# Two-layer decode block: two folded weight chunks as one transfer each, and some projection rows placed later

## The chip, the cores and the metric

The kernel runs on one core of a Trainium2 chip. Its time is the device time of one execution in microseconds (us), from a program that is launched once and reads all of its inputs from device memory. The core has five engines that this text names: PE (TensorE, matmuls; PEld are its weight loads), DVE (VectorE), ACT (ScalarE), POOL (GpSimd) and SP (SyncE, which here only issues transfers). Transfers run on 16 DMA engines beside them.

## The reference

Two blocks, A (attention over a cache) and B (a small MLP), are applied in turn, and the pair is run twice with the same weights and the same cache. The activation has 8 batch rows of one token with 448 numbers.

```python
x = x + _A_ref(_layernorm(x), A_k_cache, A_v_cache, A_wq, A_wo)
x = x + _B_ref(_layernorm(x), B_w1, B_w2, B_w3, B_w4)
x = x + _A_ref(_layernorm(x), A_k_cache, A_v_cache, A_wq, A_wo)
x = x + _B_ref(_layernorm(x), B_w1, B_w2, B_w3, B_w4)

def _A_ref(x, k_cache, v_cache, wq, wo):     # x: 8 x 1 x 448
    q = (x @ wq).reshape(B, Sq, 16, 256)      # 16 query heads, 8 cache heads, 4096 positions
    scores = einsum("bhqd,bhkd->bhqk", q, k) * 256 ** -0.5
    o = einsum("bhqk,bhkd->bhqd", softmax(scores), v)
    return o.reshape(B, Sq, 4096) @ wo

def _B_ref(x, w1, w2, w3, w4):                # one token: the shifted groups are zero
    x1 = x + hs
    return x1 + _gelu(_layernorm(x1) @ w3) @ w4
```

With one token per row, the four groups of B's first part are shifted out of the sequence, so `hs` is zero and `w1` and `w2` are not read. K and V of one batch row and one cache head are 4096 x 256 numbers of bf16, 2 MB each; there are 8 x 8 such pairs. Both layers use the same cache.

## The kernel before

**Rows and layers.** The kernel works through the batch rows. For each row b it runs layer 0 (all 8 cache heads) and then layer 1 on the same cache. Heads 0 to 2 are the "free" heads: their K and V are loaded once for each layer. Heads 3 to 7 are "kept": parts of their K (head 7: one quarter) and of V (heads 6 and 7) stay on chip from layer 0 to layer 1, and layer 1 begins with them.

**Cache slots.** The cache lives in 30 slots of 512 KB (`QUARTERS`); a K or V tile of 2 MB is four units. SP loads one to four neighbouring units by one transfer, if that many neighbouring slots are free. A slot comes free when PE has used the unit for the last time, by a score (L1136 or L1378) or by the product with the probabilities (L1262).

**One head.** `front` loads K, turns it by PE (L1482) with copies back by DVE and ACT (L1413, L1414), scores it with the two queries (L1378 by rows, L1136 by columns), and makes the softmax's probabilities. `back` loads V, multiplies (L1262), copies out (L1276, L1278), sums (L1286), scales into `oT` (L1292, two buffers) and multiplies by the head's part of `wo`: `wo_row`, four matmuls on L1312, which add to one row of the PSUM tile `psR`. When most heads of a row (seven, as a rule) have been added, `turn` (L1074, L1077) turns the row into a column.

**The MLP.** After layer 0's attention of row b, `mid(b)` runs block B on one column: L907 (`w3`), L1053 (`w4`), then the second layer's queries (L891, `wq`). Beside that chain run the backs of the next row's free heads, whose V is loaded in single units (`MOST = 1`).

**The weights.** 448 = 3 x 128 + 64. The last 64 rows of `wq` (4096 columns) and `w3` (1792 columns) are folded: their left half lies in partitions 0 to 63 of `wqx_sb` and `w3x_sb`, their right half in 64 to 127. Each half is a transfer of its own (L1546 to L1549, L1556, L1557); the second half of `wq`'s is issued by ACT, everything else that is large by SP (L626 for weights, L643 for the cache).

**The order of the work.** It is not written by hand. Every operation is handed to a planner (`Plan.schedule`) with an estimated duration and a priority, the smaller the earlier. `CH` puts the chain operations first, `hi` (the operation's number less 100,000) comes next, and scores and most products have their own number. The planner walks a model of the engines in time and fixes the order on each engine; the waits are derived from it. For the cache loads it keeps SP's order and chooses when each load is issued, how many units it joins and in which slots. `next_kv` waits for as many neighbouring free slots as the load would like, until `LEAD` (3.5 us) before the modelled end of what is already queued; then it takes the largest fit that there is. `ISSUE` (4.0 us) is the modelled time from an issue to the first data. While PE would idle, the planner places filler matmuls (L1689).

Of the kernel before, what the change touches and what calls it, by code (L numbers as in the profile page):

```python
# [6 lines left out]
P = 128  # L7
B = 8
D = 448
# [43 lines left out]
Q1 = 176  # L53
ROWS = True
SHORT = 0.1


class Op:
# [28 lines left out]
class Plan:  # L87
# [5 lines left out]
    HOT = 3500  # L93


    ISSUE, LEAD = 4.0, 3.5
    BLOCK, FETCH = 128, 6.0
    LAT = {"pe": 0.25, "dve": 0.06, "act": 0.06, "pool": 0.05, "sp": 0.4}

# [374 lines left out]
def bass_interleave_layers__gqa_block_cached__mixer_s_mlp__decode_kernel(  # L474
# [20 lines left out]
    plan = Plan()  # L495
# [6 lines left out]
    def sb(name, shape, dt):  # L502
        n = 4 if dt in (f32, i32) else 2
        for s in shape[1:]:
            n *= s
        al = 32 if n >= 128 else 8
        cursor[0] = (cursor[0] + al - 1) // al * al
        t = nc.alloc_sbuf_tensor_at(name, shape, dt, offset=cursor[0], align_bytes=al)
        cursor[0] += (n + al - 1) // al * al
        assert cursor[0] <= high0, (name, cursor[0], high0)  # L510
        return t

    wq_sb = sb("wq_sb", [P, 3, 4096], bf)
    wqx_sb = sb("wqx_sb", [P, 2048], bf)
    wo_sb = sb("wo_sb", [P, 32 * D], bf)
    w3_sb = sb("w3_sb", [P, 3, F], bf)
    w3x_sb = sb("w3x_sb", [P, F // 2], bf)
# [105 lines left out]
    def dma(name, dst, src, nbytes, sem, val, wr, at, row=8192):  # L623

        us = nbytes / 16 / 26.88e3 + nbytes / row / 16 * 0.008
        plan.op("sp", lambda eng: eng.dma_start(dst, src), us / FASTER, name, wr=wr, prio=at,  # L626
                dma=(sem, val))

    def dma_once(name, parts, keys, at, also=()):

        for i, (dst, src, nbytes, *row) in enumerate(parts):
            dma(name, dst, src, nbytes, nc.alloc_semaphore(f"s_{name}{i}"), 16,
                [keys[i], *(also if i == 0 else ())], 4 * at - 0.5, *row)
# [3 lines left out]
    def issue_kv(o, n, q):  # L637
# [6 lines left out]
        o.dma = (slot_sem[q], 16 * slot_n[q])  # L644
        o.dur = ((n << 15) / 26.88e3 + 8 * 0.008) / FASTER + SHORT * (n < 3)

# [36 lines left out]
    def const_c(v):  # L683
# [7 lines left out]
            wr=["sel"])  # L691
# [7 lines left out]
    for bank, key in [(psR, "R"), (psM, M)]:  # L699
        plan.op("dve", lambda v, bank=bank: v.memset(bank[:, :], 0.0), 0.5, "const",  # L700
                wr=["psM", ("row", 0), ("row", 1)], banks=[key])
    for i in range(2):
        plan.op("dve", lambda v, i=i: v.memset(psP[i][:, 0:DH], 0.0), 0.3, "const", wr=["pz"],
                banks=[f"P{i}"])
# [9 lines left out]
    def pe(fn, n, rd=(), wr=(), banks=(), name="chain", prio=None, width=20):  # L714

        if prio is None:
            prio = urge[0] + len(plan.ops)
        d = 0.06 + 0.026 * n
        return plan.op("pe", fn, (d, max(d, 0.06 + n * width / 1200), width * n, n), name, rd=rd, wr=wr, banks=banks, prio=prio)
# [152 lines left out]
    def q_mms(t, mts, rhs, bank, at, step, copies):  # L872

        last = None
        for i, mt in enumerate(mts):
            hq, c = mt // 2, mt % 2
            for kc in range(4):


                if kc < 3:
                    w = wq_sb[:, kc, hq * 256 + c:hq * 256 + 256:2]
                    r = rhs(kc)
                else:
                    o = (hq % 8) * 256
                    w = wqx_sb[:, o + c:o + 256:2]
                    r = rhs(3 + hq // 8)
                if step == 1:
                    r = bcast(r, copies, 1)  # L890
                last = t.matmul(bank[:, at + i * step:at + i * step + copies], w, r,  # L891
                                start=(kc == 0), stop=(kc == 3))
        return last

    def h_mms(t, rhs, bank, at, step, copies, mts=range(14)):

        last = None
        for mt in mts:
            for kc in range(4):

                g = mt % 7
                c = slice(g // 2 * 256 + g % 2, g // 2 * 256 + 256, 2) if g < 6 else slice(768, 896)
                w = w3_sb[:, kc, mt // 7 * 896:mt // 7 * 896 + 896][:, c] if kc < 3 else w3x_sb[:, c]
                r = rhs(kc if kc < 3 else 3 + mt // 7)
                if copies > step:
                    r = bcast(r, copies // step, 1)
                last = t.matmul(bank[:, at + mt * step:at + mt * step + copies], w, r,  # L907
                                start=(kc == 0), stop=(kc == 3))
        return last

    W4 = ["w40", "w41", "w42", "w43"]
    W3 = ["w30", "w31", "w32", "w3x0", "w3x1"]

    def column_sums():

# [2 lines left out]
        for g in range(4):  # L918
            pe(lambda t, g=g: q_mms(t, range(8 * g, 8 * g + 8), one, psM, SC, 1, QW), 32,
               rd=["mask"] + WQ, wr=["psM"], banks=[M], prio=len(plan.ops), width=QW)  # L920

# [5 lines left out]
    def column_sums_h():  # L927
        def one(kc):
            return mask[:, kc:kc + 1]
        pe(lambda t: h_mms(t, one, psM, SC, 1, HW), 56, rd=["mask"] + W3, wr=["psM"], banks=[M],  # L930
           prio=len(plan.ops), width=HW)
        dv(lambda v: v.tensor_single_scalar(cs_h[:, :], psM[:, SC:SC + 14], 1.0 / D, ALU.mult), rd=["psM"], wr=["cs_h"], banks=[M],
           prio=len(plan.ops))

    WQ = ["wq0", "wq1", "wq2", "wqx0", "wqx1"]

    def last_rows(src, skey, n):

# [37 lines left out]
    def mlp(src, skey, n, dst, dkeys, rows_open=False):  # L976
# [12 lines left out]
        if dst is None:  # L989
            shift(0, mom[:, 2, 2:3], rsy[:, 1, B - 2:B - 1], [("s", 0), ("y", 1, B - 2)])  # L990
            last_stats(1)
            pe(lambda t: h_mms(t, lambda kc: src[:, kc, 2:2 + n], ch, at, n, HW // 2), 56,
               rd=[*skey] + W3, wr=[kb], banks=[bk], width=HW)
            for r in range(n):
                scaled(r, rsy[:, 1, B - 2 + r:B - 1 + r], [("y", 1, B - 2 + r)])
        elif few:
# [9 lines left out]
            for mts in H_PARTS:  # L1006
                pe(lambda t, mts=mts: h_mms(t, lambda kc: src[:, kc, 0:n], ch, at, n, HW, mts), 4 * len(mts),
                   rd=[skey] + W3, wr=[kb], banks=[bk], width=HW)
            variance(st, False, v0, ["st"], "v0", sbank)
# [4 lines left out]
        else:  # L1014
            norm(src, skey, True, n)
            pe(lambda t: h_mms(t, lambda kc: yb6[:, kc, 0:n], ch, 0, n, n), 56,
               rd=KH + W3, wr=[kb], banks=[bk])
            dv(lambda v: v.tensor_copy(h_, ch[:, 0:m]), rd=[kb], wr=KH, banks=[bk])
# [217 lines left out]
    def back(layer, b, h):  # L1236
# [10 lines left out]
        hi = len(plan.ops) - 10 ** 5  # L1247
# [6 lines left out]
        for u in range(4):  # L1254

            def pv(t, u=u, q=vs[u]):
                last = None
                for s in range(8):
# [10 lines left out]
                    wr=[("pv", par, x) for x in range(u, 4)], banks=[bk], prio=first)  # L1269
            if u == 0:  # L1270
                o.tbank = bk
            if u not in keep_v:
# [7 lines left out]
                banks=[bk], prio=hi)  # L1280

        def sum_mm(t):
# [8 lines left out]
           prio=hi)  # L1291
# [3 lines left out]
            wr=[("oT", no)], banks=[bk], prio=hi).tbank = bk  # L1295
# [10 lines left out]
        if k <= turn_at:  # L1306
            def wo_row(t):
                last = None
                for i in range(4):
                    a = (4 * h + i) * D  # L1310
                    r = 64 * layer + 32 * (i % 2)
                    last = t.matmul(psR[r:r + 1, 0:D], oT[no][:, i % 2, i // 2:i // 2 + 1],  # L1312
                                    wo_sb[:, a:a + D], start=(k == 1 and i < 2),
                                    stop=(k == turn_at and i >= 2),
                                    skip_group_check=True, tile_position=(0, r))
                return last
            o = plan.op("pe", wo_row, (0.41, 0.78, 448, 4), "wor", rd=[("oT", no), "wo0"], wr=[kr],
                        banks=["R"], prio=hi)
            if k == HOTK and layer == 0:
                o.hot = True  # L1320
        xkeys = [ok] + (["x3all" if b < B - 2 else ("xf", b - B + 2)] if layer else [])
        if k == turn_at:
            for a, mts in [(0, range(2)), (2 * P, range(2, NC5))]:
                w = min(2 * P, D - a)
                dv(lambda v, a=a, w=w: v.tensor_copy(oW[:, 0, 0:w], psR[:, a:a + w]), 0.42, rd=[kr],
                   wr=REG, banks=["R"], name="acc", prio=hi)
# [4 lines left out]
                def turn(t, a=a, mts=mts):  # L1331
# [7 lines left out]
                   prio=hi, width=YW)  # L1339
# [188 lines left out]
    def second_queries(b, h, prio):  # L1528

        src = x2c[b % 2]  # L1530
        pe(lambda t: q_mms(t, range(4 * h, 4 * h + 4), lambda kc: src[:, kc, 0:1], psM, SC,
                           1, QW), 16, rd=[("x2", b)] + WQ, wr=["psM"], banks=[M], prio=prio, width=QW)
        dv(lambda v: v.scalar_tensor_tensor(
# [9 lines left out]
    def load_wq():  # L1543
        dma_once("wq", [(wq_sb[:, kc, :], A_wq[kc * P:(kc + 1) * P, :], 1 << 20)
                        for kc in range(3)], ["wq0", "wq1", "wq2"], 2)
        dma_once("wqx", [(wqx_sb[0:64, :], A_wq[384:D, 0:2048], 1 << 19)], ["wqx0"], 0.05)  # L1546
        s_wqx = nc.alloc_semaphore("s_wqx1")
        plan.op("act", lambda a: a.dma_start(wqx_sb[64:P, :], A_wq[384:D, 2048:4096]), 0.1, "wqx1",
                wr=["wqx1"], prio=0, dma=(s_wqx, 16))  # L1549

    def load_rest():
        dma_once("wo", [(wo_sb[:, :].rearrange("p (t n) -> p t n", n=2 * D),
                         A_wo.rearrange("(t m c) n -> m t (c n)", m=P, c=2), 3670016, 1792)], ["wo0"], 6)
        dma_once("w3", [(w3_sb[:, kc, :], B_w3[kc * P:(kc + 1) * P, :], 458752)
                        for kc in range(3)], ["w30", "w31", "w32"], 18)
        dma_once("w3x", [(w3x_sb[0:64, :], B_w3[384:D, 0:896], 114688 * 2),  # L1556
                         (w3x_sb[64:P, :], B_w3[384:D, 896:1792], 114688 * 2)], ["w3x0", "w3x1"], 18)  # L1557
    def load_w4():
        w4s = B_w4.rearrange("(s f) n -> s f n", s=2)
        dma_once("w4", [(w4_sb[:, 7 * i * D:(7 * i + 6) * D].rearrange("p (t n) -> p t n", n=2 * D),  # L1560
# [5 lines left out]
    def first_queries():  # L1566
# [11 lines left out]
        for h in range(8):  # L1578
            pe(lambda t, h=h: q_mms(t, range(4 * h, 4 * h + 4), lambda kc: yb[:, kc, :], psM,
                                    Q1 + 32 * h, B, B), 16, rd=YB + WQ, wr=["psM", "q1"], banks=[M])  # L1580
        first_q(0, None)
# [4 lines left out]
    free_heads = list(range(HKV - KEEP_K))  # L1586
# [19 lines left out]
    def run(tasks):  # L1606
        for t in tasks:
            (fronts_of if t[0] == "f" else back)(*t[1:])
# [31 lines left out]

    load_wq()
    load_rest()
    first_queries()
    load_w4()
# [104 lines left out]
```

## Time and profile before

| what | value |
|---|---|
| median of 3 runs | 1085.01 us (1085.01 to 1085.93) |
| the profiled execution's own time | 1082.09 us |
| its span, first to last instruction | 1080.2 us |
| mean granted TensorE clock | 0.937 |
| busy: PE, PEld, DVE, ACT, POOL | 943.6, 651.1, 598.8, 339.3, 97.9 us |
| read from device memory | 434.18 MB |
| cache loads of SP: 2 MB, 1.5 MB, 1 MB, 512 KB | 137, 25, 22, 141 |
| projection rows on PE (L1312) | 444 matmuls, 65.1 us |

A profile is one execution. The page gives busy time and share for each engine, then the span in 40 slices of 27 us, with the busy share in tenths, the DMA engines' share and what they moved. "DMA queue" lines give packets, megabytes and the time that the packets took as a share of 16 engines. "DMA issues" lines give transfer, issuing queue, count, size and the median time from issue to landing. A wait line reads: who waited, for whom, us in total, times, the longest. In a timeline line the first two numbers are start and length in us. A line number such as L1312 is a line of the kernel before.

### The profile page before, as it was taken

Reading aid. Unit: us, or ns where it says so; the run is one execution under the profiler, and the core shown is the slowest. Engines: PE = TensorE matmul, PEld = TensorE weight load, DVE = VectorE, ACT = ScalarE, POOL = GpSimd, SP = SyncE. Lnnn points to the kernel's source line nnn. Section 1 sums busy time; section 2 is a strip of 40 time slices with the busy share of each in tenths; the row PEclk is TensorE's granted clock in tenths of the full one; section 3 lists DMA queues with packets and bytes.
Section 4 is the critical chain, followed back from the end, with each engine's and each line's share of the span. In section 5 each row is a group of like instructions: output and inputs, shape, how many; then the busy total and the mean of one; then the engine's idle time right before and its main releaser. Section 6 shows DMA issues by size and latency. Waiting matters only on the chain.

```text
span 1080.2 us, 33935 instructions
## 1 busy us (share of the span) xinstructions
PE 943.6 (87%) x15144; PEld 651.1 (60%) x15144; DVE 598.8 (55%) x1895; ACT 339.3 (31%) x940; POOL 97.9 (9%) x278
## 2 busy tenths in 40 slices
PE   5889798988988889898898989998889999998895
PEld 4556556665656656566566655666556675666663
DVE  3345445555665556455565555565556655565564
ACT  1235113341234403254023531334214341343150
POOL 0000000000110101011010100101001000110010
PEclk9899989998999989999899998999989997999895
DMA  9999999999999999999999999999999999999994
GB/s 356 407 428 420 392 380 424 426 397 410 388 425 425 421 404 413 424 427 418 385 409 427 423 415 388 427 425 423 402 389 426 426 407 398 399 427 418 348 422 189
DMA packets 51342, 436.38 MB, mean 404 GB/s; under 512 B 5486, under 2 KB 8700, under 8 KB 27260
## 3 DMA queue, kind: packets, MB, share of 16 engines
q1 hardware_dynamic: 51108, 433.95, 97.9%
q8 instruction: 119, 1.95, 0.7%
q10 hardware_dynamic: 88, 0.26, 0.1%
q14 instruction: 27, 0.22, 0.1%
HBM read 434.18 MB, written 0.01 MB: 402 GB/s over the span
## 4 chain that ended last, share of the span: by engine, by line
DMA 50%; PE 39%; DVE 5%; issue 2%; SPq 1%; ACT 1%; POOL 0%; POOLq 0%; DVEq 0%
DMA kv<-in_A_k_cache_dram 27%; DMA kv<-in_A_v_cache_dram 22%; PE psT L1482 14%; PE psP L1262 7%; PE psT L1378 6%; PE psM L1136 3%; PE psM L891 2%; PE psR L1312 2%; PE psM L1053 1%; SPq L626 1%; DMA w_sb<-in_B_w_dram 1%; DVE kv L1413 1%; DVE oS L1276 1%; DVE oS L1278 1%; PE psP L1286 1%
## 5 line engine op out<-in xcount | busy, mean ns | idle before, releaser
L1482 PE MATMUL psT<-ident_f,kv 128*128 128x128 f32 x2752 | 376.3, 285 | 21.6 <-DMA kv<-in_A_k_cache_dram 19.3
L1482 PEld LDWEIGHTS psT<-ident_f,kv 128*128 128x128 f32 x2752 | 305.7, 144 | 101.2 <-issue 55.2
L1413 DVE COPY kv<-psT 128x512 f32<-128x512 f32 x381 | 260.8, 690 | 180.9 <-PE psT L1482 173.3
L1414 ACT COPY kv<-psT 128x512 f32<-128x512 f32 x339 | 197.5, 586 | 389.4 <-PE psT L1482 301.1
L1262 PE MATMUL psP<-kv,pT 128*2 128x256 bf16 x4096 | 178.3, 289 | 17.9 <-DMA kv<-in_A_v_cache_dram 14.5
L1378 PE MATMUL psT<-kv,qz 128*32 128x512 bf16 x1664 | 135.9, 399 | 6.3 <-ACT kv L1414 4.0
L1262 PEld LDWEIGHTS psP<-kv,pT 128*2 128x2 bf16 x4096 | 85.0, 83 | 62.1 <-DMA kv<-in_A_v_cache_dram 27.1
L1216 POOL PARTITION_ALL_REDUCE gm<-pm x128 | 45.4, 354 | 763.1 <-DVE pm L1214 754.2
L1276 DVE CAST oS<-psP 128x256 bf16<-128x256 f32 x128 | 53.9, 421 | 65.2 <-PE psP L1262 64.5
L1226 ACT ACTIVATE pT<-sS,nb,fac 128x32 bf16<-128x32 bf16 x128 | 52.6, 417 | 115.3 <-DVE nb L1220 115.3
L1312 PE MATMUL psR<-wo_sb,oT 128*1 128x448 bf16 x444 | 65.1, 377 | 9.9 <-DVE oT L1292 3.8
L1230 POOL PARTITION_ALL_REDUCE Db<-rs x128 | 51.0, 398 | 185.7 <-ACT pT L1226 185.7
L1286 PEld LDWEIGHTS psP<-sel,oS 128*128 128x128 bf16 x512 | 23.7, 99 | 61.4 <-DVE oS L1278 57.2
L1286 PE MATMUL psP<-sel,oS 128*128 128x2 bf16 x512 | 32.1, 166 | 31.9 <-DVE oS L1278 30.3
L1378 PEld LDWEIGHTS psT<-kv,qz 128*32 128x32 bf16 x1664 | 35.3, 96 | 40.3 <-issue 12.4
L1226 ACT ACTIVATE pT<-sS,nb 128x32 bf16<-128x32 bf16 x128 | 40.8, 326 | 59.2 <-DVE nb L1220 59.2
L1689 PE MATMUL psP<-ident_f 128*128 128x256 bf16 x357 | 58.2, 286 | 0.0
L1278 DVE TENSOR_TENSOR oS<-psP,oS 128x256 bf16<-128x256 f32 x128 | 54.1, 423 | 2.9
L1393 DVE CAST sr<-psT 128x512 bf16<-128x512 f32 x51 | 35.2, 691 | 31.9 <-PE psT L1378 31.7
L1136 PEld LDWEIGHTS psM<-qz,kv 128*128 128x128 bf16 x1344 | 41.2, 99 | 18.8 <-issue 5.8
L1136 PE MATMUL psM<-qz,kv 128*128 128x48 bf16 x1344 | 47.8, 187 | 5.4 <-DVE kv L1413 3.4
L1394 ACT CAST sr<-psT 128x512 bf16<-128x512 f32 x53 | 31.0, 585 | 53.4 <-PE psT L1378 53.4
(190 smaller groups left out, 778.8 us busy)
## 6 DMA issues: line engine op xcount, KB each, us to landing
kv<-in_A_k_cache_dram SPq DMA_DIRECT2D x73, 2048.0 KB, 22.2
kv<-in_A_v_cache_dram SPq DMA_DIRECT2D x64, 2048.0 KB, 19.0
kv<-in_A_v_cache_dram SPq DMA_DIRECT2D x130, 512.0 KB, 8.5
kv<-in_A_v_cache_dram SPq DMA_DIRECT2D x14, 1536.0 KB, 9.0
kv<-in_A_k_cache_dram SPq DMA_DIRECT2D x11, 1536.0 KB, 17.3
kv<-in_A_v_cache_dram SPq DMA_DIRECT2D x14, 1024.0 KB, 7.2
kv<-in_A_k_cache_dram SPq DMA_DIRECT2D x8, 1024.0 KB, 8.0
kv<-in_A_k_cache_dram SPq DMA_DIRECT2D x11, 512.0 KB, 14.1
```

Source lines behind the costliest of these rows:

```text
L1136: last = t.matmul(ps[:, SB + 2 * i:SB + 2 * i + 2 * REP], a()[:, c:256:2], bcast(rhs(c), REP, 1), start=(c == 0), stop=(c == 1))
L1226: return a.activation(pT[nr][:, :, :].rearrange("p i j -> p j i")[:, jj, :], sview[:, jj, :], ACT.Exp, bias=nb[nm][:, jj:jj + 1], scale=sc ...
L1262: last = t.matmul(ps[g4:g4 + 2, PV0:PV0 + DH], pT[nr][:, k, :], slot_ap(q, s * 256, 256), start=(i < 4), stop=(i >= 28), skip_group_check= ...
L1276: plan.op("dve", lambda v: v.tensor_copy(oS[:, 0, :], po), 0.36, "o", rd=[("pv", par, x) for x in range(4)], wr=["oS0"], banks=[bk], prio=hi)
L1278: plan.op("dve", lambda v: v.tensor_tensor(oS[:, 1, :], po, oS[:, 0, :], ALU.subtract), 0.36, "o", rd=["oS0"] + [("pv", par, x) for x in r ...
L1286: last = t.matmul(ps[:, PV1 + 2 * c:PV1 + 2 * c + 2], oS[:, w, c:DH:2], sel[:, :], start=(w == 0), stop=(w == 1))
L1312: last = t.matmul(psR[r:r + 1, 0:D], oT[no][:, i % 2, i // 2:i // 2 + 1], wo_sb[:, a:a + D], start=(k == 1 and i < 2), stop=(k == turn_at ...
L1378: last = t.matmul(psT[bank][32 * g:32 * g + 32, :], qz[:, a:a + 32], slot_ap(qs[g // 2], g % 2 * 1024, 1024)[:, c:1024:2], start=(half == ...
L1413: return e.tensor_copy(dst, psT[bank][:, :])
L1414: return e.copy(dst, psT[bank][:, :])
L1482: last = t.transpose(psT[bank][:, s * P:(s + 1) * P], src, ident_f[:, :])
L1689: return t.matmul(dst, ident_b, bcast(ident_b[:, 0:n // 4], 4, 1), start=True, stop=True)
```

## The change

Four edits. The two folded chunks are loaded by one transfer each: the source is viewed as 2 halves x 64 rows x columns, the destination is the whole tile of 128 partitions. In the built kernel the load of `wqx_sb` has a source of 2 x 64 x 2048 elements and a destination of 128 x 1 x 2048; that of `w3x_sb` 2 x 64 x 896 and 128 x 1 x 896. Both are issued by SP, and ACT issues none. The lists `WQ` and `W3`, which say what the readers wait for, get one entry less. `LEAD` goes from 3.5 to 5.0 us. And the projection rows of the free heads in layer 0, for every row but the first, get a priority of their own number plus 100 in place of `hi`.

```diff
+WOR_AFTER = 100
...
-    ISSUE, LEAD = 4.0, 3.5
+    ISSUE, LEAD = 4.0, 5.0
...
-    W3 = ["w30", "w31", "w32", "w3x0", "w3x1"]
+    W3 = ["w30", "w31", "w32", "w3x0"]
...
-    WQ = ["wq0", "wq1", "wq2", "wqx0", "wqx1"]
+    WQ = ["wq0", "wq1", "wq2", "wqx0"]
...
             o = plan.op("pe", wo_row, (0.41, 0.78, 448, 4), "wor", rd=[("oT", no), "wo0"], wr=[kr],
-                        banks=["R"], prio=hi)
+                        banks=["R"], prio=len(plan.ops) + WOR_AFTER if layer == 0 and b and h in free_heads else hi)
...
-        dma_once("wqx", [(wqx_sb[0:64, :], A_wq[384:D, 0:2048], 1 << 19)], ["wqx0"], 0.05)
-        s_wqx = nc.alloc_semaphore("s_wqx1")
-        plan.op("act", lambda a: a.dma_start(wqx_sb[64:P, :], A_wq[384:D, 2048:4096]), 0.1, "wqx1",
-                wr=["wqx1"], prio=0, dma=(s_wqx, 16))
+        dma_once("wqx", [(wqx_sb[:, :], A_wq[384:D, :].rearrange("p (a n) -> a p n", a=2), 1 << 19)], ["wqx0"], 0.05)
...
-        dma_once("w3x", [(w3x_sb[0:64, :], B_w3[384:D, 0:896], 114688 * 2),
-                         (w3x_sb[64:P, :], B_w3[384:D, 896:1792], 114688 * 2)], ["w3x0", "w3x1"], 18)
+        dma_once("w3x", [(w3x_sb[:, :], B_w3[384:D, :].rearrange("p (a n) -> a p n", a=2), 114688 * 2)], ["w3x0"], 18)
```

All else in the changed kernel's order follows from these through the planner. Its cache loads are 127 of 2 MB, 12 of 1.5 MB, 34 of 1 MB and 196 of 512 KB.

## The prediction

> **What bounds the kernel now.** I read the page's slices and DMA queues first, then the DMA issues, then stretches of 20 to 30 us, then what the DMA queue of SP waits for, and last the start.
>
> ```profile
> DMA  9999999999999999999999999999999999999994
> GB/s 356 407 428 420 392 380 424 426 397 410 388 425 425 421 404 413 424 427 418 385 409 427 423 415 388 427 425 423 402 389 426 426 407 398 399 427 418 348 422 189
> DMA packets 51342, 436.38 MB, mean 404 GB/s; under 512 B 5486, under 2 KB 8700, under 8 KB 27260
> ...
> q1 hardware_dynamic: 51108, 433.95, 97.9%
> ...
> q10 hardware_dynamic: 88, 0.26, 0.1%
> ```
> The 16 DMA engines are busy from the first slice to the last; PE at 87% is not the bound. So the time is what the engines have to move, and work laid on one engine counts as much as work laid on all. The packet counts also show how a transfer is dealt out. Queue 10 is ACT's: its 88 packets are 64 rows of the weight chunk with 16 completion packets of 4 bytes, and 4 rows of an output with 4 completions. The 5486 small packets are 16 of data (128 and 224 bytes) and 5470 completions, which is exactly 340 transfers x 16, two loads of 8 rows x 8, one store of 6 rows x 6 and two stores of 4 rows x 4. One completion per engine: a transfer with 64 or 128 outer rows uses 16 engines, one with 8, 6 or 4 only that many.
>
> ```profile
> kv<-in_A_k_cache_dram SPq DMA_DIRECT2D x73, 2048.0 KB, 22.2
> ...
> kv<-in_A_v_cache_dram SPq DMA_DIRECT2D x130, 512.0 KB, 8.5
> ...
> wqx_sb<-in_A_wq_dram ACTq DMA_DIRECT2D x1, 256.0 KB, 3.8
> wqx_sb<-in_A_wq_dram SPq DMA_DIRECT2D x1, 256.0 KB, 4.0
> w3x_sb<-in_B_w_dram SPq DMA_DIRECT2D x2, 112.0 KB, 12.0
> ```
> These are the issues: count, size, median us to landing. Every pair in this list has the same outer row count on its source and its destination.
>
> ```profile
> 260.00:280.00 20.00, 18.99 (x445) 12.02 (x446) 10.93 (x55) 1.27 (x5) 0.35 (x1) 0.74 0.99 364
> 320.00:340.00 20.00, 16.71 (x200) 11.65 (x201) 11.71 (x31) 7.37 (x18) 1.50 (x4) 1.00 1.01 428
> 520.00:550.00 30.00, 27.87 (x615) 17.56 (x608) 17.31 (x77) 5.97 (x22) 2.61 (x7) 0.83 1.00 379
> ```
> Last column GB/s, before it the DMA share. With 2 MB loads the engines move 428 GB/s; where the free heads' V comes in 512 KB pieces around the MLP they move 364 to 379 at the same busy share.
>
> ```profile
> SPq L643 <- PE psP L1262: 631.4, 137, 25.6
> SPq L643 <- PE psT L1378: 106.6, 40, 10.1
> SPq L643 <- PE psM L1136: 69.5, 30, 7.8
> ```
> SP waits for PE to free cache slots. That costs only where the queue behind it runs short.
>
> ```profile
> 0.72 0.74 SPq L626 DMA_DIRECT2D x_row<-in_A_x_dram  x2
> 1.51 0.57 SPq L626 DMA_DIRECT2D wqx_sb<-in_A_wq_dram  x1
> 2.12 1.59 SPq L643 DMA_DIRECT2D kv<-in_A_k_cache_dram  x2
> ```
> The chunk stands ahead of everything large in SP's queue, so what delays it on an engine delays all loads on that engine.
>
> From the trace's packet records: a 4096-byte packet takes 168 ns mean (159 median), 1792 bytes 79 (76), 16384 bytes 624 (614). From its landing times, the gap between neighbouring landings is 4.91 us median (5.01 mean) for 2 MB, 3.72 (3.97) for 1.5 MB, 2.50 (2.69) for 1 MB, 1.28 (1.34) for 512 KB.
>
> **The change, part by part.** The sum is made on the profiled execution (span 1080.2, its own time 1082.09 us); the median of the runs, 1085.01, is 2.9 above it, and I add the difference to the median.
>
> *wqx in one transfer.* The destination is 128 rows, but the source is 2 x 64 rows: its outermost count is 2. No row of before has two unlike counts. With 16 engines the load costs what 512 KB costs; if the count that fits both sides decides, two engines carry 64 packets each. I take two: sixteen shares of 8 rows would have to be addressed inside the second source dimension, two shares are the outer steps of both sides. The Trainium skill, "DMA: Bandwidth & Descriptors", section "Why a DMA increments its semaphore by 16 and not by 1", says the same of unlike sides: the engine count is the largest up to 16 that divides the slowest dimension of both. By it the sum is the one below, against it the first rival's; the completion counts above agree with it for like sides.
> Price on two engines: the chunk's first packet on SP's queue starts at 3.13 us in the trace. 64 x 168 ns = 10.75 us, then the first K tile's 8 packets x 614 ns = 4.9: landing at 18.8 where it lands now at 12.14, so +6.65. Bounds: 159 ns gives 18.2 (+6.1); the 266 ns that ACT's chunk packets average at the start give 25.1 (+12.9). I take 168, because most of the 64 run after 6 us, when packets are at their later speed. The other 14 engines run ahead, but a tile has landed only with its last engine, and slots come free only after that; two engines then have no idle time to catch up in, since the mean engine idles 5.2 us between 20 and 1060 us. The chunk itself is first read at 25.3 us and needs no cover.
> ACT's issue (0.57 us) goes; ACT is idle until 17.56 anyway: nothing.
>
> *w3x in one transfer.* Now both halves take 0.57 + 0.40 = 0.97 us of landing gap. On two engines: 64 x 79 ns = 5.07, so +4.1 (76 ns: +3.9). On sixteen: 8 x 76 ns = 0.61, so -0.36. SP saves one issue of 0.5 us at 107 us with 10 us queued: nothing. PE's column sums at 119.6, which wait 1.8 us for this chunk now, wait longer, and behind them the products that free slots; that is the same 4.1, not another.
>
> *LEAD 5.0.* In the built kernels the cache loads go from 325 to 369: 512 KB pieces 141 to 196, 1 MB 22 to 34, 1.5 MB 25 to 12, 2 MB 137 to 127. By median gaps 1000.2 to 1003.0 us, +2.75; by means +4.4. I take the medians, since the means hold the stalls priced next. 44 more SP issues of 0.33 to 0.45 us stand in SP's own waiting.
> What it can give back: 50 loads (the first K tile left out) were issued with less than 5 us of landings ahead of them. They exceed their medians by 14.6 us, against 0.065 us each for the 274 others; 11.3 us hang on the short queue, 11.2 of the 14.6 being in the 30 loads of several units. These are what the splitting breaks up. Bounds 0 and -11.3.
>
> *Projection rows behind scores.* Of the free heads' 21 rows (PE L1312, 4 matmuls and 4 weight loads, 65.1 us / 111 = 0.59 us each), in six of seven rounds one or (in four) two come to stand behind the first 64 score matmuls, L1136, in the built order. Slots of kept K come free up to 1.2 us earlier. This is paid from the same 11.3 us. What could be late is the third head's oT write, since oT has two buffers; the wait is at most one row per round, so 7 x 0.59 = +4.1 at most and nothing at least. For both parts I take -4.5, about 40% of the pool: the split loads still wait for PE.
>
> Sum: 6.65 + 4.1 + 2.75 - 4.5 = +9.0: span 1089, and 1094.0 against the median.
>
> **The rivals.**
> *Sixteen engines after all.* Then the start lies between +1.0 (ACT's head start: its chunk packets begin at 2.09, SP's at 3.13) and -1.7 (the first K tile lands 6.60 us after the chunk, where 2 MB take 4.91); the middle is -0.35. With w3x -0.36, LEAD +2.75 and the pool -4.5 that is -2.5, or 1082.5. For it: the destination's 128 rows; slow halves, 0.97 us where 0.61 would do. Against it: the source's outer 2. The Trainium skill, "SBUF — State Buffer", Door 1, says 64 partitions reach half of the ports; this speaks for the folding, and the 0.97 agrees, but it says nothing of how the source is cut.
> *Two engines, and nothing from the pool.* The 512 KB stretches stall although they are single pieces already (3.4 of the 14.6 us), so finer pieces may only cost: 10.75 + 4.4 = +15.2, or 1100.2.
> *Two engines, lag worked off.* If the 5.2 us of idle time is free for those two, 10.75 - 5.2 + 2.75 - 4.5 = +3.8, or 1088.8. Against it: idle comes where slots are missing, and then no engine has work.
>
> **How the numbers follow.** Forecast 0.62, sixteen engines 0.18, nothing from the pool 0.12, lag worked off 0.08. With two engines the bounds are 6.1 + 3.9 + 2.75 - 11.3 = +1.5 and 12.9 + 4.1 + 4.4 + 4.1 = +25.5, ends that need every term at its end; 0.82 of the chance lies mostly between 1087 and 1101. The range 1082 to 1101 adds the better half of the sixteen-engine case. A measurement tells 0.2%, 2.2 us, from no change: sixteen engines give faster in 0.11, same in 0.05, slower in 0.02; the others same in 0.03, slower in 0.79.
>
> **What would show it.** Small packets: 6130 under 512 B if both chunks run on two engines (380 loads x 16, the same 30, two chunks x 2, 16 of data), 6158 if on sixteen. wqx to landing 12 us or more instead of 4, w3x about 16 instead of 12; the first K tile landing near 18.8. If these hold and the time is still near 1085, the pool was larger than 11.3 us or the lag does not last. If the short stretches (260 to 280, 520 to 550, moved by the shift) still show 364 to 379 GB/s, the pool gave nothing. The rows on PE: L1312 behind the first L1136 in six rounds, with oT's waits on it no more than now. The prediction is wrong at its root if 16 completions follow each folded chunk.

## The result, and the profile after

The changed kernel takes 1095.91 us (median of 4 runs, 1094.09 to 1097.87) where the kernel before took 1085.47 (1085.01 to 1086.10): a ratio of 1.0093, 95% interval 1.0074 to 1.0112. The forecast was 1094.0 with a range of 1082 to 1101. The profiled execution has a span of 1094.7 us, 14.5 above that of before; of these, 4.0 are the two executions themselves (1096.53 us is 0.6 above its kernel's median, 1082.09 is 3.4 below).

From the page of the changed kernel, the slices and queues:

```profile
DMA  8989999999999999999999999999999999999994
GB/s 284 411 367 412 332 345 420 425 423 419 386 427 426 421 389 397 428 423 421 399 415 426 426 418 379 426 424 425 404 398 424 426 417 391 412 423 418 326 415 199
DMA packets 57618, 436.39 MB, mean 399 GB/s; under 512 B 6130, under 2 KB 9344, under 8 KB 34944
...
q1 hardware_dynamic: 57464, 434.21, 97.7%
...
q10 hardware_dynamic: 8, 0.00, 0.0%
```

6130 small packets is the number that the prediction gave for two engines on each folded load; sixteen would have left 6158. ACT's queue has only the output row left (4 packets and 4 completions). The first, third, fifth and sixth slice are slow: 284, 367, 332 and 345 GB/s where before had 356, 428, 392 and 380. All of the loss lies in the first 165 us.

From the list of issues, with count, size and median us to landing where the view finds one:

```profile
kv<-in_A_k_cache_dram SPq DMA_DIRECT2D x67, 2048.0 KB, 24.8
...
kv<-in_A_v_cache_dram SPq DMA_DIRECT2D x170, 512.0 KB, 8.5
...
wq_sb<-in_A_wq_dram SPq DMA_DIRECT2D x3, 1024.0 KB, 32.3
...
wqx_sb<-in_A_wq_dram SPq DMA_DIRECT2D x1, 512.0 KB
w3x_sb<-in_B_w_dram SPq DMA_DIRECT2D x1, 224.0 KB
```

The two folded loads have no landing time: the view wants 16 completions for a transfer, and they have two. The wq loads, 18.1 us from issue to landing before, take 32.3, since they are queued behind wqx.

The stretches at the start (the last column is GB/s, before it the DMA share, before that the clock), first of before, then of after:

```profile
3.00:8.00 5.00, 0.00 (x0) 0.00 (x0) 0.00 (x0) 0.00 (x0) 0.00 (x0) 1.00 0.94 280
8.00:21.00 13.00, 8.16 (x81) 7.53 (x82) 6.42 (x27) 1.76 (x3) 0.28 (x1) 1.00 0.99 415
40.00:60.00 20.00, 15.05 (x262) 8.70 (x260) 5.30 (x20) 3.09 (x11) 1.15 (x3) 0.91 1.03 404
```

```profile
3.00:8.00 5.00, 0.00 (x0) 0.00 (x0) 0.00 (x0) 0.00 (x0) 0.00 (x0) 1.00 0.97 287
8.00:21.00 13.00, 1.39 (x41) 1.25 (x41) 3.01 (x21) 0.00 (x0) 0.28 (x1) 1.00 0.99 278
40.00:60.00 20.00, 18.08 (x289) 11.21 (x287) 8.14 (x26) 5.30 (x16) 1.88 (x5) 0.75 0.88 334
274.00:294.00 20.00, 19.00 (x429) 12.18 (x428) 10.82 (x55) 2.66 (x8) 0.73 (x2) 0.74 1.00 378
534.00:564.00 30.00, 28.73 (x656) 19.23 (x657) 17.57 (x80) 5.61 (x20) 2.61 (x7) 0.89 1.02 399
```

Two things are to be seen. From 8 to 21 us the engines are as busy as before (0.99) and move a third less, 278 against 415 GB/s: the packets are slower, and not only those of two engines. From 40 to 60 us the share falls to 0.88: by the packet records 16 engines are at work up to 55 us, but only two to six between 56 and 60. The last two rows are the stretches that moved 364 and 379 GB/s before, shifted by 14 us; they now move 378 and 399.

What the other engines wait for can be read from SP's timeline, first of before, then of after:

```profile
12.29 34.30 SPq L643 DMA_DIRECT2D kv<-in_A_k_cache_dram  x1
```

```profile
23.62 35.22 SPq L644 DMA_DIRECT2D kv<-in_A_k_cache_dram  x1
```

The issue of the K load behind `wo_sb` lasts until 46.6 us before and until 58.84 us after. It waits for no semaphore, and only 24 of the 30 slots were given out before it, so it isn't slots that are missing. In each of the 13 traces it ends 0.7 to 1.1 us behind the landing of the last cache load ahead of `wo_sb` (58.14 us here), so it comes as late as that landing does. What holds it there no run shows. Meanwhile the other engines run through all that was issued.

The landing times of the cache loads put numbers to it. The first K tile lands at 26.07 us (12.14 before): +13.9. At the 76th of the 808 units, just behind w3x, the kernel is 17.6 us late, at the 93rd 15.5, and from there it stays between 10 and 17 to the end, 14.2. From the last landing to the end it is 12.6 us, as before (12.3).

For w3x there is a wait on PE; from the waits of the changed kernel (who waits, for whom, us, times, longest):

```profile
DVE cs_h L933 <- PE psM L908: 8.1, 1, 8.1
PE psM L908 <- DMA w3x_sb<-in_B_w_dram: 7.2, 1, 7.2
```

Before, PE waited 1.8 us in that place.

### The profile page after: what moved, and what is told of

Read it like the earlier page. It is cut to its first block, busy times and chain, and to the rows that moved or that the text cites. A ratio compares the mean times of both kernels' runs of the same rounds, so it can differ in the third digit from the quotient of the medians.

```text
span 1094.7 us, 33979 instructions
## 1 busy us (share of the span) xinstructions
PE 946.4 (86%) x15138; PEld 648.1 (59%) x15138; DVE 596.3 (54%) x1892; ACT 342.2 (31%) x943; POOL 97.9 (9%) x278
## 2 busy tenths in 40 slices
DMA packets 57618, 436.39 MB, mean 399 GB/s; under 512 B 6130, under 2 KB 9344, under 8 KB 34944
## 4 chain that ended last, share of the span: by engine, by line
DMA 55%; PE 37%; DVE 5%; issue 1%; SPq 1%; ACT 1%; POOL 0%; DVEq 0%
DMA kv<-in_A_k_cache_dram 33%; DMA kv<-in_A_v_cache_dram 18%; PE psT L1483 12%; PE psP L1263 8%; PE psT L1379 5%; DMA wq_sb<-in_A_wq_dram 3%; PE psM L1137 3%; PE psM L892 2%; PE psR L1313 2%; PE psM L1054 1%; DMA w_sb<-in_B_w_dram 1%; DVE oS L1279 1%; PE psP L1287 1%; DVE kv L1414 1%; SPq L627 1%
## 5 line engine op out<-in xcount | busy, mean ns | idle before, releaser
L1414 DVE COPY kv<-psT 128x512 f32<-128x512 f32 x371 | 254.9, 691 | 197.8 <-PE psT L1483 191.0
L1415 ACT COPY kv<-psT 128x512 f32<-128x512 f32 x349 | 203.6, 587 | 398.8 <-PE psT L1483 319.3
L1263 PEld LDWEIGHTS psP<-kv,pT 128*2 128x2 bf16 x4096 | 81.1, 82 | 63.3 <-DMA kv<-in_A_v_cache_dram 22.3
L1313 PE MATMUL psR<-wo_sb,oT 128*1 128x448 bf16 x444 | 61.7, 362 | 6.4 <-DVE oT L1293 3.3
L1394 DVE CAST sr<-psT 128x512 bf16<-128x512 f32 x55 | 38.1, 692 | 32.3 <-PE psT L1379 32.2
L1137 PEld LDWEIGHTS psM<-qz,kv 128*128 128x128 bf16 x1344 | 43.8, 102 | 16.6 <-issue 7.9
L1137 PE MATMUL psM<-qz,kv 128*128 128x48 bf16 x1344 | 50.9, 191 | 2.9 <-DVE oT L1293 1.3
L1210 DVE CAST sS<-psM 128x64 bf16<-128x64 f32 x128 | 28.1, 219 | 32.5 <-PE psM L1137 24.5
## 6 DMA issues: line engine op xcount, KB each, us to landing
kv<-in_A_v_cache_dram SPq DMA_DIRECT2D x60, 2048.0 KB, 18.7
```

What stands on the lines that cost most here:

```text
L1137: last = t.matmul(ps[:, SB + 2 * i:SB + 2 * i + 2 * REP], a()[:, c:256:2], bcast(rhs(c), REP, 1), start=(c == 0), stop=(c == 1))
L1263: last = t.matmul(ps[g4:g4 + 2, PV0:PV0 + DH], pT[nr][:, k, :], slot_ap(q, s * 256, 256), start=(i < 4), stop=(i >= 28), skip_group_check= ...
L1414: return e.tensor_copy(dst, psT[bank][:, :])
L1415: return e.copy(dst, psT[bank][:, :])
```

## The experiments

All ratios are to the kernel before on the same chip, with 95% intervals. In four of them (all with "flat") the weight rows of the folded chunks land in the wrong partitions, so that the same work is done on rows in another order. Where an edit changes what the planner reckons with, it also joins the cache loads anew: before has 325 of them, the changed kernel 369, and where a kernel below has another number it is given.

**Is it the source's outer count?**

```diff
-A_wq[384:D, :].rearrange("p (a n) -> a p n", a=2)
+A_wq[384:D, :].rearrange("p (a n) -> (p a) n", a=2)
 (and the same for B_w3)
```

> The changed kernel with one thing else: the source of both folded loads is read as 128 rows one after the other (row 2r+a to partition 2r+a), so that its outermost count is 128 and not 2. Same bytes, same destination, same order of all instructions; the weight rows land in the wrong partitions, so the output isn't the reference's. Two-engine theory: both loads are spread over 16 engines again, 6158 packets under 512 B, the first K tile lands near 12 us and not at 26.1, and the time falls by the 13.9 and 5.5 us that the two loads cost, plus about 0.4 for w3x that now takes 0.6: near 1076 to 1079 us. Rival that one transfer over 128 partitions is what costs, however the source is cut: it stays near 1096. Rival that the smaller cache loads cost the time: it stays near 1096 too, with the first K tile near 12.

Measured: 1077.16 us (1075.81 to 1079.66), ratio 0.992 (0.9895 to 0.9944). From its page and its issues:

```profile
DMA packets 57646, 436.39 MB, mean 406 GB/s; under 512 B 6158, under 2 KB 9372, under 8 KB 34972
...
wqx_sb<-in_A_wq_dram SPq DMA_DIRECT2D x1, 512.0 KB, 3.9
w3x_sb<-in_B_w_dram SPq DMA_DIRECT2D x1, 224.0 KB, 12.2
```

Nothing else differs from the changed kernel, neither the destination, the bytes, the number of transfers nor the place of one instruction, and with 28 more completion packets (2 x 14) it takes 18.8 us less (1.0093 - 0.9920 = 1.73% of 1086). The first K tile lands at 10.8 us. The rivals that one transfer costs by itself, or that the smaller cache loads do, fall. Nor is it the addresses of the source, which the flat view takes in another order: the half loads of before read the same pieces as the changed kernel and land in 4 us. The Trainium skill, "DMA: Bandwidth & Descriptors", section "Why a DMA increments its semaphore by 16 and not by 1", states the rule that the prediction weighed, the largest engine count up to 16 that divides the slowest dimension of both sides. The 6130 and 6158 agree with it, also for unlike sides (2 and 128).

**The other parts without the folds, and the folds without the other parts.** The first kernel is the one before with `LEAD` 5.0 and the moved rows (361 cache loads); the second has the folds alone (337).

```diff
-    ISSUE, LEAD = 4.0, 3.5
+    ISSUE, LEAD = 4.0, 5.0
 (and the priority of the free heads' rows; the four half loads stay)
```

> The kernel before with LEAD 5.0 and the moved projection rows, and its four half loads as they were. Two-engine theory: what is left of the change is its gain, which the two traces put at 19.4 - 14.2 = 5.2 us: near 1080 us (1078 to 1083). By the recorded sum without the loads, 2.75 - 4.5 = -1.75: 1083.7. Rival that finer loads cost: 1088 or more.

Measured: 1079.54 us (1078.52 to 1083.18), ratio 0.9942 (0.9923 to 0.9961). It beats both kernels, and no part of the computation is left out or changed. Against it the folds of the changed kernel cost 16.4 us (1.0093 - 0.9942 = 1.51%).

```diff
-    ISSUE, LEAD = 4.0, 5.0
+    ISSUE, LEAD = 4.0, 3.5
 (in the changed kernel, with prio=hi for the rows again)
```

> The kernel before with the two folded loads alone. Two-engine theory with the prices read from the trace after: +13.9 and +5.5, so near 1104 us (1100 to 1106); with the recorded prices 6.65 + 4.1: 1096. Rival that the lag of two engines is worked off in the stalls: 1090 or less. The first K tile lands at about 26 us, w3x adds about 6.4 us in front of the next landing.

Measured: 1106.53 us (1100.63 to 1112.67), ratio 1.019 (1.0142 to 1.0239). First K tile at 24.9 us. The change is a loss by the folds, of 1.5% beside the other parts and 1.9% alone, and a gain of 0.6% by the rest.

**LEAD or the moved rows?** They have 371 and 331 cache loads.

```diff
 (kernel before, one at a time)
-    ISSUE, LEAD = 4.0, 3.5
+    ISSUE, LEAD = 4.0, 5.0
```

> The kernel before with LEAD 5.0 alone (371 cache loads). If the gain of the two parts (half loads kept: 0.994 of before) is LEAD's, 1079 to 1082 us; if it is the moved rows', no change or, by the recorded price of finer loads alone, +2.75 to +4.4.

Measured: 1080.84 us (1077.03 to 1085.70), ratio 0.994 (0.9917 to 0.9963).

```diff
-                        banks=["R"], prio=hi)
+                        banks=["R"], prio=len(plan.ops) + WOR_AFTER if layer == 0 and b and h in free_heads else hi)
```

> The kernel before with the moved projection rows alone (331 cache loads). If LEAD brings the gain, within 1.5 us of before; if the earlier scores do, 1080 to 1083 us.

Measured: 1087.04 us (1084.57 to 1090.73), ratio 1.0007 (0.9984 to 1.0029). The gain is LEAD's; the rows behind the scores are worth nothing that can be measured (within 0.3%).

**Does LEAD work where the prediction put it, and is there more to be had?**

```diff
-    ISSUE, LEAD = 4.0, 3.5
+    ISSUE, LEAD = 4.0, 6.5
```

> The kernel before with LEAD 6.5 (388 cache loads; 325 with 3.5, 371 with 5.0). With 5.0 alone the ratio was 0.994. If the queue still runs short in places with 5.0, 6.5 gains again: 0.990 to 0.993, near 1077. If 5.0 has taken what there was (the loads with less than 5 us ahead of them exceed their medians by 11 us in that run, most of it in single pieces), the 17 more loads change nothing: 0.993 to 0.996.

Measured: 1080.17 us (1078.68 to 1081.63), ratio 0.9949 (0.9928 to 0.9970): no more than with 5.0. The landing times of the profiled executions suggest what it works on. I counted, as for the prediction, the cache loads that were issued with less than 5 us of landings ahead of them, and by how much they exceed the median gaps of before:

| kernel | LEAD | loads of several units: number, surplus in us | all such loads: number, surplus in us |
|---|---|---|---|
| before | 3.5 | 30, 11.2 | 50, 14.6 |
| rows only | 3.5 | 25, 12.1 | 44, 16.9 |
| folds only | 3.5 | 24, 12.3 | 52, 21.9 |
| LEAD only | 5.0 | 8, 4.4 | 38, 11.4 |
| halves, LEAD and rows | 5.0 | 9, 1.6 | 38, 8.1 |
| changed kernel | 5.0 | 6, 2.0 | 50, 8.7 |
| changed kernel, flat | 5.0 | 4, 2.6 | 37, 7.6 |
| LEAD 6.5 | 6.5 | 2, 0.3 | 38, 3.9 |

With 3.5 a large load waits for several slots while the queue runs out, 11 to 12 us in all; with 5.0 it is split and most of that is gone. The five kernels below that are not in the table fall in the same groups (26 loads and 10.6 us with 3.5; 4 to 11 loads and 1.5 to 3.2 us with 5.0). With 6.5 the rest goes too, but the time stays. By the median gaps the 17 further splits cost only about 1 us, so why it stays isn't shown. (The first K tile, and the loads behind a w3x or a later wqx on two engines, are left out. Single executions differ by 3 us and more, so only the two groups are to be compared, not neighbours in the table. That of LEAD alone was with 1085.70 us the slowest of its ten, slower than the profiled one of before, although its surplus is smaller: the surplus isn't the whole time.)

**What does one even transfer gain?** The folds alone, from a source of 128 rows, with LEAD 3.5 (337 cache loads).

```diff
 (folds only, as above)
-rearrange("p (a n) -> a p n", a=2)
+rearrange("p (a n) -> (p a) n", a=2)
```

> The kernel before with both folded loads as one transfer each from a source of 128 rows in a row, LEAD 3.5, and nothing else (the rows land in the wrong partitions). It tells what one transfer over 128 partitions is worth when 16 engines carry it: by the recorded rival -0.35 and -0.36, so 0.999; by the first K tile's 1.3 us and w3x's 0.4, 0.998. With two engines the same kernel had 1.019.

Measured: 1087.77 us (1081.03 to 1091.82), ratio 1.0008 (0.9987 to 1.0030). The first K tile lands 1.65 us earlier than before, but nothing of it is left in the time. Against the same kernel with two engines (1106.53) it is 18.8 us faster (19.8 by the ratios), as much as in the pair with LEAD 5.0. With LEAD 5.0 and the moved rows the flat folds take 1077.16 us and the half loads 1079.54, on the same chip: 2.4 us, but the intervals of the two ratios overlap. In both comparisons with half loads the cache loads differ (337 to 325, 369 to 361). So folding two 64-row loads into one is worth between nothing and some 2 us here when 16 engines carry it.

**Why was wqx dearer than predicted?** Its 64 packets on each of two engines start at 2.96 us and end at 20.36, 272 ns apiece (by their own records 254 on average), where 168 had been taken. The first test moves the load behind the three large wq loads (361 cache loads).

```diff
-1 << 19)], ["wqx0"], 0.05)
+1 << 19)], ["wqx0"], 2)
```

> The changed kernel with the folded wq load issued behind the three large wq loads and not ahead of the first K tile. Asks why its 64 packets per engine took 282 ns each and not 168. If it is the start of the program that is slow, they take 159 to 170 ns here, 10.5 us, and the time is 6 to 7 us below the changed kernel's, near 1089. If packets of two engines slow down whenever the other engines write beside them, they take 250 ns or more again and the time is the same as the changed kernel's within 3 us.

Measured: 1097.80 us (1095.33 to 1100.10), ratio 1.0104 (1.0074 to 1.0135). The packets run from 21.70 to 38.17 us, 257 ns apiece. It is not the start of the program. The second test has SP wait until the folded load has landed, so that it runs alone.

```diff
-            o = plan.op("sp", None, 0.0, "kv", wr=[("s", x, 0), ("s", x, 1)], prio=loads[0])
+            o = plan.op("sp", None, 0.0, "kv", rd=["wqx0"] if loads[0] == 0 else [], wr=[("s", x, 0), ("s", x, 1)], prio=loads[0])
```

> The changed kernel, where SP waits for the folded wq load to land before it issues the first K tile; all else in the same order. Fourteen engines idle meanwhile. If the 282 ns of its packets come from the other engines' writes beside them, they take about 159 ns now, the load lands near 13.5 us, the first K tile near 20 (1.6 us from issue to data, 4.9 us of data) instead of 26.1, and the kernel with more idle time is the faster by 5 to 6 us: near 1090. If two engines are slow by themselves, the load lands near 21, the first K tile near 28, and the time is 2 us worse than the changed kernel's, near 1098.

Measured: 1091.53 us (1088.97 to 1093.83), ratio 1.0037 (1.0015 to 1.0059). Its timeline (start, length in us) and SP's wait, and its stretch with the load alone:

```profile
1.51 0.67 SPq L627 DMA_DIRECT2D wqx_sb<-in_A_wq_dram  x1
14.53 0.83 SPq L644 DMA_DIRECT2D kv<-in_A_k_cache_dram  x2
```

```profile
SPq L644 <- DMA wqx_sb<-in_A_wq_dram: 12.3, 1, 12.3
```

```profile
3.00:14.00 11.00, 1.34 (x41) 1.25 (x41) 0.87 (x7) 0.00 (x0) 0.28 (x1) 1.00 0.12 47
```

Share 0.12 is two of sixteen engines, and 47 GB/s is what two move. Alone they need 11.2 us (2.96 to 14.13), 174 ns a packet. Fourteen engines stand still for 11 us, and the kernel is 4.4 us faster than with them working (6.1 by the ratios, whose intervals allow 3 to 9): the first K tile lands at 22.33 instead of 26.07. So the packets of the two are slowed by the loads beside them, and the loads beside them by the two (16 KB packets between 3 and 13 us: 905 ns mean in the changed kernel, 635 with the flat source). Which resource they share isn't shown. The Trainium skill, "SBUF — State Buffer", Door 1, has 16 ports of 8 partitions each. Two engines that write all 128 partitions might cross the ports of the others; no run here separates ports from other causes.

**Which load costs how much?**

```diff
 (changed kernel, one load at a time)
-A_wq[384:D, :].rearrange("p (a n) -> a p n", a=2)
+A_wq[384:D, :].rearrange("p (a n) -> (p a) n", a=2)
```

> The changed kernel with the folded wq load read as 128 rows in a row, and w3's still as 2 x 64 (the wq rows land in the wrong partitions). Splits the two prices: two engines for w3's load alone should leave 5.5 to 6.1 us of the 18.7 between the changed kernel and the one with both loads flat, so near 1083 us; with the recorded price, 4.1 + 0.4, near 1081.7. Its small packets are 6144 (one load on 16 engines, one on 2).

Measured: 1079.52 us (1078.65 to 1082.46), ratio 0.9928 (0.9900 to 0.9956), 6144 small packets. The expectation was missed: w3 on two engines leaves 2.4 us (1079.52 - 1077.16), not 5.5.

```diff
-B_w3[384:D, :].rearrange("p (a n) -> a p n", a=2)
+B_w3[384:D, :].rearrange("p (a n) -> (p a) n", a=2)
```

> The changed kernel with w3's folded load read as 128 rows in a row, and wq's still as 2 x 64 (the w3 rows land in the wrong partitions). With wq's load flat, taking w3's to 16 engines gained only 2.4 us at the end, although the lag at its place was 4.7 to 6.2. If it is worked off later, it is here too: 1 to 3 us below the changed kernel, near 1093.5. If the two prices add, 5 to 6 us below, near 1090.

Measured: 1089.48 us (1086.40 to 1091.16), ratio 1.0040 (1.0024 to 1.0056): 6.4 us below the changed kernel, near the 1090 that the expectation gave if the prices add. But with wqx flat it had been only 2.4. The medians side by side:

| us | w3 on 16 engines | w3 on two | w3's price |
|---|---|---|---|
| wq on 16 engines | 1077.16 | 1079.52 | 2.4 |
| wq on two | 1089.48 | 1095.91 | 6.4 |
| wq's price | 12.3 | 16.4 | both 18.7 |

The four kernels ran on several chips. By the ratios to before w3 costs 0.9 and 5.8 us and wq 13.0 and 17.9, each to within 3 to 4 us, so that the prices do not simply add is likely, but at the edge of what the runs tell.

Against the flat kernel the one with w3 alone on two engines is 4.7 us late at the 76th unit, 6.2 at the 88th, 4.1 at the 278th, 0.8 at the 774th and 2.4 at the last: most of its lag is worked off. In the pair with wq on two engines the difference stays at 6 to 8.4 us from the 76th unit on. Why the one lag goes and the other stays isn't settled. What the traces show is that SP's issue behind `wo_sb` ends at 57 to 60 us in each kernel with wq on two engines, and at 44 to 47 us in the others.

A layout of the chunks in which the flat source puts the rows where they belong would have to change the activations, the mask and the output columns too; it wasn't tried. The fastest kernels whose rows all lie where the reference has them are the three with half loads and LEAD 5.0 or 6.5, at 0.994 to 0.995.

## Why the prediction was right, and where it was not

- **What bounds the kernel**: right. Work laid on two engines alone made the whole kernel later, as "work laid on one engine counts as much as work laid on all" said; for wqx by 12.3 us or more, for w3x alone by less than its lag. The lag was to last because slots come free only with the last engine; in the first stretch in which most engines had no work, 56 to 60 us, it was SP's hanging issue and not slots.
- **Two engines**: right, to the packet (6130), and shown by the flat source. The rival of sixteen engines falls, which had 0.18; its own price for an even transfer, -0.35 and -0.36 us, is below what the flat folds let be seen (1.0008 +- 0.0022 with LEAD 3.5, 2.4 us below the halves with 5.0).
- **wqx, +6.65 with bounds +6.1 and +12.9**: mis-sized. The first K tile came 13.9 us late, beyond the upper bound, and the load costs 12.3 to 16.4 us of time against a flat one. The step that failed is "I take 168, because most of the 64 run after 6 us, when packets are at their later speed". That speed is one of 16 engines which each carry a sixteenth; two that carry a whole load beside fourteen others have 257 to 272 ns. The row nearest in kind was the 266 ns at the start (262 by the records of ACT's 64 packets), which the prediction had as its upper end.
- **w3x, +4.1**: at its place 6.4 us of landing gap beyond 2 MB's median, 98 ns a packet instead of 79; 6.4 us of time in the changed kernel, 2.4 with wqx flat. Mis-sized by the same step, a mean over the whole trace: the half loads of w3x themselves had 104 ns in the trace of before.
- **LEAD +2.75 and pool -4.5, net -1.75**: the direction was right, the size too small. Measured net: -0.6%, 6.5 us, by LEAD alone. Of the 11.2 us on loads of several units 9.2 are gone in the changed kernel, where about 40% of the pool had been taken on the ground that split loads still wait for PE. In part they do: the surplus of the single units grew from 3.4 to 6.7 us, so that 5.9 of the 14.6 are given back. With the 2.75 for finer loads that makes about 3 of the 6.5 us; where the rest comes from isn't shown.
- **Projection rows**: nothing, 1.0007. Waits of `oT` on the rows did not grow (3.1 us, once; 5.1 before), so the +4.1 bound was not called on, and the earlier slots brought nothing either.
- **The sum, +9.0**: it measured +10.4. Against the half loads, as the sum has it, the folds cost +16.4 instead of +10.75, and the rest gave -6.3 instead of -1.75: errors of 5.7 and 4.5 us that nearly cancel. That the total was closer than its terms is luck. The sum was made on the profiled execution of before; between the two profiled executions the span grew by 14.5.
- **The other rivals**: "nothing from the pool" (1100.2) falls by LEAD's ratio. "Lag worked off" is wrong for wqx, whose lag stays to the end, and mostly true for w3x when it is alone.
- **What was to show it**: wqx 12 us or more (it was 19.9, from issue to its second completion) and the first K tile near 18.8 (it was 26.1); the short stretches above 364 and 379 GB/s (378 and 399), so that the pool did give something.

## What to carry to other kernels

Before two half transfers are folded into one, look at the outermost count of both sides as the built kernel has them: a source of 2 x 64 rows turns 16 engines into two, and in a kernel bound by its transfers those two set the time. Count the completion packets in a profile: 16 for each transfer, or it is not spread. And when a change bundles a loss with a gain, run each alone: here one constant of the planner was worth 0.6%, hidden under a loss of 1.5%.

## What the runs showed of the hardware that was not expected

- A transfer on two engines takes 174 ns per 4096-byte packet alone, and 257 to 272 ns beside loads on the other engines, whose own 16 KB packets grow from 635 to 905 ns on average. Letting fourteen engines stand still for 11 us was 4.4 us faster than letting them work.
- One issue of SP hangs for 33 to 36 us in each of the 13 traces without a semaphore to wait for, and ends 0.7 to 1.1 us behind the landing of an earlier load. In the changed kernel two late engines thus left the others without work for some 4 us.
- SP's issues slow down behind such a transfer: by SP's timelines (below, first of the changed kernel, then with the flat source) the three issues of `wq_sb` take 4.96 us in the changed kernel, 1.52 with the flat source and 1.63 where SP waited for wqx to land first, and the issue of `wo_sb`, with the same loads ahead of it, starts at 18.00 us and at 6.36 (before: 8.40, where SP issued half of wqx and ACT the other).

```profile
3.19 4.96 SPq L627 DMA_DIRECT2D wq_sb<-in_A_wq_dram  x3
18.00 5.57 SPq L627 DMA_DIRECT2D wo_sb<-in_A_wo_dram  x1
```

```profile
2.85 1.52 SPq L627 DMA_DIRECT2D wq_sb<-in_A_wq_dram  x3
6.36 3.67 SPq L627 DMA_DIRECT2D wo_sb<-in_A_wo_dram  x1
```
